# Sliding-window attention with a top-1 mixture of experts on one core: another order of the first steps, another layout of the turned keys and queries, and a later write of empty rows

## The chip, the cores and the metric

One core of a Trainium2 chip runs the whole program. The metric is the device time of one execution in microseconds (us); three timed executions of the kernel before gave 647.55, 648.55 and 649.33 us, median 648.55 us. The engines are named as in the profile: PE (TensorE; PEld is its weight load), DVE (VectorE), ACT (ScalarE), POOL (GpSimd), SP (SyncE, which here only issues DMAs). "SPq" and "ACTq" are rows of DMA issues on these two engines.

## The reference, cut to what matters

```python
# q, k, v: [8 batches, 8 heads, 576 positions, 64]
scores = (q @ k.transpose(0, 1, 3, 2)) / 8
mask   = (rel >= 0) & (rel < 64)            # rel = query position - key position
scores = where(mask, scores, -1e9); scores -= max(scores)
attn   = exp(scores); attn /= sum(attn) + 1e-9
x      = (attn @ v), heads side by side      # 4608 tokens x 512
logits = x @ w_gate + modality_bias[modality_id]
e      = argmax(logits); gate = softmax(logits)[e]
out    = gate * (relu(x @ w1[e]) @ w2[e])    # 8 experts, 512 -> 1024 -> 512
```

## The kernel before, in words

**Tiles and steps.** The 4608 tokens are 72 blocks of 64 positions. One step s of the main loop takes a pair of blocks (128 tokens, 36 pairs) through one stage each: in step s the scores of pair s are formed, the probabilities of pair s-1 are turned, the values of pair s-2 are summed and its result turned, the gate logits of pair s-3 are taken. Since a window reaches back over one block only, a block of queries meets two blocks of keys.

**Turned keys and queries.** Keys and queries are loaded in groups of four blocks (two pairs), turned by PE with an identity matrix into PSUM (L439, called from `heads_t`), and copied by DVE or ACT into `kT` and `qT` (L539, `heads_out`). Both tiles hold eight blocks as a ring: groups alternate between its two halves. Before, their free axes are `[pair of heads, block of the ring, position]`, so that one group's blocks are spread over the whole tile in four pieces. The first group is loaded in two halves (a pair of blocks each, keys by SP, queries by ACT, each in two loads, for even and odd positions) and turned by `first_heads` (copies at L551); `first_pair(0)` stands ahead of the loop, `first_pair(1)` in step 0.

**Order.** The code is scheduled by hand: each engine runs its instructions in the order in which the program issues them, and an engine that waits holds up everything behind it in its own queue. What an instruction waits for is worked out from the tiles that it touches. A step issues, in this order: `values` and `values_out` of pair s-2 (PE L615; DVE reciprocal L621 and product `xa` L623), `logits` of pair s-3 (PE L640, DVE L645), `scores` (PE L563, 16 products into the PSUM tiles `sp0`, `sp1`), `minima` (eight DVE instructions, L577, each adds the mask and takes a row's minimum), `swap_v`, `probs_t` of pair s-1 (PE, copies `pT` by ACT L598), the exponentials (ACT L589, eight, in three lots), `x_t`, the next group's heads in two lots (PE L439 and copies L539), small routing and table instructions on DVE ("ticks"), and the expert weights (`weights`, from step 3: one SP load and its split by ACT L111 and DVE L116).

**swap_v.** The values product needs block 2p-1 and 2p in one tile `ve`: its upper 64 rows are copied by DVE from the pair before (L502), its lower 64 by POOL from this pair (L503). Both copies of pair s-1 are issued in step s behind the minima. `vo`, the loaded values, has three buffers, `ve` two, `sp` and `av` one each.

**Routing.** From step 5 on, every second step routes a group of two pairs: at its end the DVE has the row numbers, and POOL scatters 2 x 128 token rows into `xs_scratch` in DRAM (L716). POOL runs in order too: the scatters stand ahead of the next `ve` copy. From step 12 (`FIRST`) the expert products (L279, L301) are interleaved with the attention steps on PE, and after step 38 they run alone to the end.

**Small inputs.** The modality numbers (`mod_i`, L820), the bias rows (`brow`, L822) and the gate weights (`wg`, L825) are loaded by ACT ahead of its first copy. POOL casts the modality numbers (L912), PE turns them once (the 36-row product of L439, at the end of step 0), DVE copies the result (L916), and POOL forms `bias_sel` from it (L920 to L926), ahead of the first `ve` copy in its queue.

**Empty rows.** Slots without tokens read rows of zeros with an invalid row number. They are written once, 514 KB from the tile `padrow`, by SP at the end of step 2 (L1024).

Of the kernel before, what the change touches and what calls it, by code (L numbers as in the profile page):

```python
# [19 lines left out]
P = 128  # L20
W64 = 64
# [5 lines left out]
def tile_window_attn_moe(  # L27
# [12 lines left out]
    nc = tc.nc  # L40
# [396 lines left out]
    def turn(out_, in_, p0=0):  # L437
        n = in_.shape[0]
        nc.tensor.transpose(out=out_, in_=in_, identity=ident[p0:p0 + n, p0:p0 + n])  # L439
# [11 lines left out]
    small = actx.enter_context(tc.tile_pool(name="small", bufs=2))  # L451


    kT = att.tile([P, HP, RING, W64], F32, name="kT")
    qT = att.tile([P, HP, RING, W64], F32, name="qT")
# [6 lines left out]
    vo = {}  # L462
# [31 lines left out]

    def swap_v(p):

        e = work.tile([P, H, D], F32, name="ve", bufs=2)
        ve[p] = e
        if p == 0:
            nc.gpsimd.memset(e[W64:P], 0.0)  # L500
        else:
            nc.vector.tensor_copy(out=e[W64:P], in_=vo[p - 1][W64:P])  # L502
        nc.gpsimd.tensor_copy(out=e[0:W64], in_=vo[p][0:W64])  # L503

    def new_qk(G, nm):
        if G in AHEAD:
# [27 lines left out]
                turn(tp[:, n * P:(n + 1) * P], src[:, t, 2 * i + h])  # L534

    def heads_out(tp, G, nm, i, copy):
        pos0 = GBLK * (G % 2)
        dst = (qT if nm == "q" else kT)[:, 2 * i:2 * i + 2, pos0:pos0 + GBLK, :]
        copy(out=dst.rearrange("p h j (i t) -> p h t (j i)", t=2),  # L539
             in_=tp.rearrange("p (h t i) -> p h t i", h=2, t=2))  # L540

    def first_heads(nm, i, tp, copy):

        src = qk[0, nm].rearrange("p t (h a) d -> p t h (a d)", a=2)
        rows = slice(i * W64, (i + 1) * W64)
        for h in range(HP):
            for t in range(2):
                n = 2 * h + t
                turn(tp[:, n * W64:(n + 1) * W64], src[rows, t, h], i * W64)
        dst = (qT if nm == "q" else kT)[:, :, 2 * i:2 * i + 2, :]  # L550
        copy(out=dst.rearrange("p h j (i t) -> p h t (j i)", t=2),  # L551
             in_=tp.rearrange("p (h t i) -> p h t i", h=HP, t=2))

    def scores(p):


        g = 2 * p % RING
        win = (slice(g, g - 2 if g else None, -1 if g else RING - 1), slice(g, g + 2))
        sp = [ps_s.tile([P, 512], F32, name=f"sp{a}") for a in range(2)]
        for hp in range(HP):  # L560
            for a, c in ((0, 0), (1, 1), (0, 1), (1, 0)):
                rows = slice(a * W64, (a + 1) * W64)
                nc.tensor.matmul(  # L563
                    out=sp[a][c * W64:(c + 1) * W64, hp * P:(hp + 1) * P], lhsT=qT[rows, hp, g + c, :],
                    rhs=kT[rows, hp, win[c], :], start=True, stop=True)
# [246 lines left out]
    for f, args in at.pop(-1):  # L812
# [7 lines left out]
    nc.scalar.dma_start(out=mod_i, in_=mod_id.bitcast(I32).rearrange("(g x) -> g x", x=2 * P))  # L820
    brow = const.tile([P, 2, E], F32, name="brow")
    nc.scalar.dma_start(  # L822
        out=brow, in_=mod_bias.rearrange("(o m) e -> o m e", o=1).broadcast_to([P, 2, E]))
    wg = const.tile([P, NC1, E], F32, name="wg")
    nc.scalar.dma_start(out=wg, in_=w_gate.rearrange("(c p) e -> p c e", p=P))  # L825
    idle = epool.tile([P, 2 * 512], BF16, name="hh", bufs=2)
    nc.vector.memset(idle[:, 0:512], 0.0)

# [11 lines left out]
    nc.gpsimd.memset(kT[:, :, RING - 1, :], 0.0)  # L840


    masks = const.tile([P, 3, P], F32, name="masks")
# [81 lines left out]
            if m:  # L925
                nc.gpsimd.tensor_tensor(out=bias_sel, in0=bias_sel, in1=dst, op=ALU.add)  # L926

    def first_pair(i):
        for nm in "kq":
            first_heads(nm, i, turn_bank(0), nc.vector.tensor_copy if nm == "k" else nc.scalar.copy)  # L930

    first_pair(0)

    def weights(s):

# [10 lines left out]
    for s in range(NPR + 4):  # L946
        j = s % GB
        for f, args in at.pop(s, ()):
            f(*args)
        n_tick = 6 if s < FIRST else 5  # L950
        n_gap = 0 if s < FIRST else 4
        G = s // GB + 1
        heads = PARTS[j] if G < NG else ()
        R = (s - 5) // GB if s >= 5 and j == 1 else -1

        if 2 <= s < NPR + 2:
            values(s - 2)
            values_out(s - 2)
        if 3 <= s < NPR + 3:
            logits(s - 3, turn_bank(s))  # L960
            if (s - 3) % GB == GB - 1:
                route1((s - 3) // GB)
        if s < NPR:
            scores(s)
            if s == 0:
                keep_warm(WARM[1])
                first_pair(1)
            minima(s)
        if 1 <= s <= NPR:
# [24 lines left out]
        run_later()  # L994
        tick(n_tick)
        cnt = None
        if R >= 0:
            tp = turn_bank(s)
            rk = route2(R, tp)
            if R == NG - 1 or any(R == T for T, _ in EARLY):  # L1000
                cnt = counts_out(tab if R == NG - 1 else pl, counts(R, tp))
            route3(R, rk)
        if s < NPR:
            exps(s, (5, 6, 7))
        if n_gap > 2:
            if FIRST < s < FIRST + 3:
                weights(s)
            gap(it, True)
        if heads:
            tp = turn_bank(s)  # L1010
            heads_t(G, *heads[1], tp)
            heads_out(tp, G, *heads[1], nc.scalar.copy if heads[1] == K1 else nc.vector.tensor_copy)
        run_later()
        tick(n_tick)
        if s >= 3:
            weights(s)
        if n_gap > 3:
            gap(it, True)
        run_later()
        if s == 0:  # L1020
            select_bias()
            choose()
        if s == 2:
            nc.sync.dma_start(out=xs_blk[DUMMY:DUMMY + 2].rearrange("b p c -> p b c"), in_=padrow)  # L1024
# [270 lines left out]
```

## Time and profile before

| what | value |
|---|---|
| median of three runs | 648.55 us (647.55 to 649.33) |
| the profiled execution's own time | 648.28 us |
| its span in the profile | 646.4 us, 1.9 us less than its time |
| PE busy in the span | 620.0 us, 96% |
| DVE, ACT, POOL busy | 367.7 us, 299.4 us, 137.4 us |
| moved by DMA | 88.07 MB |

A row of the timeline gives the start in us from the span's beginning, the duration in us, engine, line, operation, output and inputs with their shapes, and in brackets how long the engine had been idle and what released it. A row of the windows gives, for a stretch, each engine's busy time and number of instructions, the clock that TensorE was granted (1.00 is full), the busy share of the DMA engines and GB/s. Matmuls are pipelined: a row's duration is that of one from start to end, and the next can begin long before.

### The profile page before, as it was taken

Reading aid. Unit: us, or ns where it says so; the run is one execution under the profiler, and the core shown is the slowest. Engines: PE = TensorE matmul, PEld = TensorE weight load, DVE = VectorE, ACT = ScalarE, POOL = GpSimd, SP = SyncE. Lnnn points to the kernel's source line nnn. Section 1 sums busy time; section 2 is a strip of 40 time slices with the busy share of each in tenths; the row PEclk is TensorE's granted clock in tenths of the full one; section 3 lists DMA queues with packets and bytes.
Section 4 is the critical chain, followed back from the end, with each engine's and each line's share of the span. In section 5 each row is a group of like instructions: output and inputs, shape, how many; then the busy total and the mean of one; then the engine's idle time right before and its main releaser. Section 6 shows DMA issues by size and latency. Waiting matters only on the chain.

```text
span 646.4 us, 17286 instructions
## 1 busy us (share of the span) xinstructions
PE 620.0 (96%) x6508; PEld 554.6 (86%) x6509; DVE 367.7 (57%) x1494; ACT 299.4 (46%) x932; POOL 137.4 (21%) x314
## 2 busy tenths in 40 slices
PE   6888889999999999999999999999999999999996
PEld 4677779898989888889998898899898999989986
DVE  2889967777767686766655365122214524757611
ACT  2789875756565646555544111111113513555411
POOL 4315330232142212320322220011011101101102
PEclk9999989999999999999999999999999999999999
DMA  9988975764876754553412124421041732677300
GB/s 164 195 186 216 212 197 132 196 161 120 181 171 153 159 144 103 144 133 82 132 51 83 50 99 171 157 67 66 23 173 45 236 113 85 218 247 227 120 1 36
DMA packets 138885, 88.07 MB, mean 136 GB/s; under 512 B 116746, under 2 KB 116784, under 8 KB 138672
## 3 DMA queue, kind: packets, MB, share of 16 engines
q1 hardware_dynamic: 130112, 67.44, 42.2%
q0 software_dynamic: 5856, 18.92, 7.8%
q10 hardware_dynamic: 2832, 0.59, 0.6%
q8 instruction: 52, 0.85, 0.6%
q14 instruction: 33, 0.27, 0.2%
HBM read 67.49 MB, written 23.91 MB: 141 GB/s over the span
## 4 chain that ended last, share of the span: by engine, by line
PE 50%; DVE 0%; ACT 0%; issue 0%; POOL 0%; POOLq 0%; ACTq 0%
PE y L301 22%; PE em L279 12%; PE sp L279 10%; PE tp L439 1%; PE y L352 1%; PE av L615 1%; PE em L254 1%; PE tp L254 1%; PE sp L327 0%; PE em L327 0%; PE tp L640 0%; PE sp L563 0%; DVE xa L623 0%; ACT ss L589 0%; DVE hl L288 0%
## 5 line engine op out<-in xcount | busy, mean ns | idle before, releaser
L301 PE MATMUL y<-Whi,hh 128*128 128x512 f32 x288 | 118.7, 412 | 0.0
L301 PE MATMUL y<-Wlo,hh 128*128 128x512 f32 x288 | 112.9, 392 | 0.0
L301 PE MATMUL y<-Whi,hl 128*128 128x512 f32 x288 | 112.8, 392 | 0.0
L589 ACT ACTIVATE ss<-ss,mn 128x128 f32<-128x128 f32 x288 | 112.5, 397 | 0.0
L279 PE MATMUL em<-xh,Whi 128*128 128x256 f32 x400 | 103.5, 293 | 1.2 <-ACT xh L192 0.7
L279 PE MATMUL em<-xh,Wlo 128*128 128x256 f32 x400 | 98.5, 280 | 0.0
L288 DVE SCALAR_TENSOR_TENSOR hl<-em,hh 128x512 fp32r<-128x512 f32 x50 | 34.5, 690 | 92.9 <-ACT hh L287 91.3
L312 POOL DMA_INDIRECT out_dram<-y,id x36 | 37.3, 1036 | 224.6 <-DVE y L309 145.9
L279 PEld LDWEIGHTS em<-xh,Whi 128*128 128x128 f32 x400 | 75.9, 190 | 2.6 <-ACT xh L192 0.9
L279 PEld LDWEIGHTS em<-xh,Wlo 128*128 128x128 f32 x400 | 75.8, 190 | 0.9
L287 ACT ACTIVATE hh<-em 128x512 fp32r<-128x512 f32 x50 | 29.6, 592 | 93.3 <-PE em L279 89.4
L577 DVE CUSTOM_DVE_ANT_0 ss<-sp,masks 128x128 f32<-128x128 f32 x288 | 63.5, 286 | 13.4 <-PE sp L563 13.4
L598 ACT COPY pT<-tp 128x512 f32<-128x512 f32 x58 | 32.2, 589 | 78.0 <-PE tp L439 78.0
L301 PEld LDWEIGHTS y<-Whi,hl 128*128 128x128 f32 x288 | 54.1, 188 | 12.3
L279 PE MATMUL em<-xl,Whi 128*128 128x256 f32 x400 | 63.4, 281 | 0.0
L301 PEld LDWEIGHTS y<-Whi,hh 128*128 128x128 f32 x288 | 54.1, 188 | 7.5
L301 PEld LDWEIGHTS y<-Wlo,hh 128*128 128x128 f32 x288 | 54.3, 188 | 7.1
L589 ACT ACTIVATION_READ_ACCUMULATOR ss<-ss,mn 128x1 f32 x288 | 55.8, 194 | 0.0
L716 POOL DMA_INDIRECT xs_scratch<-xa,idx x36 | 36.3, 1007 | 89.1 <-DVE lm L659 26.9
L279 PEld LDWEIGHTS em<-xl,Whi 128*128 128x128 f32 x400 | 54.2, 189 | 0.0
L288 DVE SCALAR_TENSOR_TENSOR hl<-sp,hh 128x512 fp32r<-128x512 f32 x22 | 15.2, 692 | 61.1 <-ACT hh L287 61.1
L615 PEld LDWEIGHTS av<-ve,pT 128*64 128x64 f32 x576 | 36.4, 138 | 15.2 <-issue 7.4
(242 smaller groups left out, 1243.6 us busy)
## 6 DMA issues: line engine op xcount, KB each, us to landing
xt<-xs_scratch SPq DMA_DIRECT2D x18, 514.0 KB, 4.0
vo<-in_v_dram SPq DMA_DIRECT2D x32, 256.0 KB, 4.1
y<-in_moe_w_dram SPq DMA_DIRECT2D x32, 256.0 KB, 4.0
vo<-in_moe_w_dram SPq DMA_DIRECT2D x24, 256.0 KB, 3.5
ss<-in_moe_w_dram SPq DMA_DIRECT2D x24, 256.0 KB, 3.8
qk<-in_k_dram SPq DMA_DIRECT2D x18, 256.0 KB, 5.5
qk<-in_q_dram SPq DMA_DIRECT2D x18, 256.0 KB, 4.9
xs_scratch<-xs_scratch SPq DMA_DIRECT2D x8, 514.0 KB, 6.0
```

Of the source, the lines that this page charges most:

```text
L254: nc.tensor.transpose(out=tp[:, n * P:(n + 1) * P].bitcast(F32R), in_=xt[:, t, c * P:(c + 1) * P].bitcast(F32R), identity=ident_r)
L279: nc.tensor.matmul(out=hb[:, i * TP:(i + 1) * TP], lhsT=w[buf][:, c0:c0 + P], rhs=x[:, c * TP:(c + 1) * TP], start=(n == 0), stop=(n == le ...
L287: nc.scalar.activation(out=hh, in_=hb, func=AF.Relu),
L288: nc.vector.scalar_tensor_tensor(out=hl, in0=hb, scalar=0.0, in1=hh.bitcast(F32), op0=ALU.max, op1=ALU.subtract)))
L301: nc.tensor.matmul(out=sl["y", t], lhsT=h[:, i * TP + t * P:i * TP + (t + 1) * P], rhs=w[buf][:, c0:c0 + DM], start=(k == 0 and n == 0), s ...
L312: ins = nc.gpsimd.indirect_dma_start(out=out, out_offset=bass.IndirectOffsetOnAxis(ap=sl["id"][:, t:t + 1], axis=0), in_=y, in_offset=None ...
L352: nc.tensor.matmul(out=yp[:, cols], lhsT=sl["h", n][lo][:, c * P:(c + 1) * P], rhs=w[buf][:, c0 + cols.start:c0 + cols.stop], start=(m == ...
L577: nc.vector.tensor_tensor_reduce(out=ss[a][:, hp, :], in0=sp[a][:, hp * P:(hp + 1) * P], in1=mask, scale=-1.0 / 8.0, scalar=3.0e38, op0=AL ...
L589: nc.scalar.activation(out=ss[a][:, hp, :], in_=ss[a][:, hp, :], func=AF.Exp, bias=mn[:, h:h + 1], scale=-1.0, accum_out=sm[:, h:h + 1])
L598: nc.scalar.copy(out=pT, in_=pp)
L615: nc.tensor.matmul(out=av[c * W64:(c + 1) * W64, 2 * hp + a], lhsT=pT[:, i:i + W64], rhs=(vo if c else ve)[p][:, 2 * hp + a, :], start=Tru ...
L716: ins = nc.gpsimd.indirect_dma_start(out=xs, out_offset=bass.IndirectOffsetOnAxis(ap=idx[:, j:j + 1], axis=0), in_=xg[j], in_offset=None)
```

## The change

Five things are edited.

1. `kT` and `qT` get the axes `[half of the ring, pair of heads, block of the group, position]`, so that a group is one contiguous half of the tile. `place(g, hp)` gives the position of a block; `win` in `scores` gives the two key blocks.
2. `first_heads` is split in two: the turns are issued by position parity (keys even, queries even, keys odd, queries odd), and for the first pair each copy is cut into halves of two head pairs, the first by DVE, the second by ACT. For the second pair the copies stay whole (keys DVE, queries ACT).
3. In step 0 the second pair's copies stand behind the eight minima (DVE) and behind five of the eight exponentials (ACT), no longer ahead of them. Its turns keep their place on PE.
4. The three small loads are issued by ACT behind the first pair's copies.
5. The upper half of `ve` (`swap_upper`, DVE) is issued at the head of a step, ahead of the reciprocal; the lower half (POOL) keeps its place. The empty rows are written at the end of step 5 in place of step 2.

```diff
-    kT = att.tile([P, HP, RING, W64], F32, name="kT")
+    kT = att.tile([P, 2 * HP * GBLK, W64], F32, name="kT")
+    def place(g, hp):
+        a, j = divmod(g, GBLK)
+        return (a * HP + hp) * GBLK + j
...
     def swap_v(p):
-        e = work.tile([P, H, D], F32, name="ve", bufs=2)
-        ve[p] = e
+        e = ve[p]
         if p == 0:
             nc.gpsimd.memset(e[W64:P], 0.0)
-        else:
-            nc.vector.tensor_copy(out=e[W64:P], in_=vo[p - 1][W64:P])
         nc.gpsimd.tensor_copy(out=e[0:W64], in_=vo[p][0:W64])
+    def swap_upper(p):
+        e = work.tile([P, H, D], F32, name="ve", bufs=2)
+        ve[p] = e
+        if p > 0:
+            nc.vector.tensor_copy(out=e[W64:P], in_=vo[p - 1][W64:P])
...
+    def first_heads_out(nm, i, tp, copies):
+        dst = by_group(qT if nm == "q" else kT)[:, 0, :, 2 * i:2 * i + 2, :]
+        n = HP // len(copies)
+        for c, copy in enumerate(copies):
+            hs = slice(c * n, (c + 1) * n)
+            copy(out=dst[:, hs].rearrange("p h j (i t) -> p h t (j i)", t=2),
+                 in_=tp.rearrange("p (h t i) -> p h t i", h=HP, t=2)[:, hs])
...
-    def first_pair(i):
-        for nm in "kq":
-            first_heads(nm, i, turn_bank(0), nc.vector.tensor_copy if nm == "k" else nc.scalar.copy)
-    first_pair(0)
+    both = nc.vector.tensor_copy, nc.scalar.copy
+    def first_pair(i, copies):
+        tps = [turn_bank(0) for _ in "kq"]
+        for t in range(2):
+            for nm, tp in zip("kq", tps):
+                first_heads_t(nm, i, t, tp)
+        for nm, tp, c in zip("kq", tps, copies):
+            first_heads_out(nm, i, tp, c)
+    first_pair(0, (both, both))
+    nc.scalar.dma_start(out=mod_i, in_=mod_id.bitcast(I32).rearrange("(g x) -> g x", x=2 * P))
+    nc.scalar.dma_start(
+        out=brow, in_=mod_bias.rearrange("(o m) e -> o m e", o=1).broadcast_to([P, 2, E]))
+    nc.scalar.dma_start(out=wg, in_=w_gate.rearrange("(c p) e -> p c e", p=P))
...
+        if 1 <= s <= NPR:
+            swap_upper(s - 1)
         if 2 <= s < NPR + 2:
             values(s - 2)
...
             if s == 0:
                 keep_warm(WARM[1])
-                first_pair(1)
             minima(s)
...
             exps(s, (2, 3, 4))
+        if s == 0:
+            first_pair(1, (both[:1], both[1:]))
...
-        if s == 2:
+        if s == 5:
             nc.sync.dma_start(out=xs_blk[DUMMY:DUMMY + 2].rearrange("b p c -> p b c"), in_=padrow)
```

How the instructions move is shown at three places. The names in brackets are the semaphores that a row waits for, one per engine or DMA lane; DMASW0 and DMASW1 are lanes of POOL's own DMAs.

ACT in step 0, before: the small loads (L820 to L825), the two copies of queries, the exponentials (L589), a copy of the next group's keys.

```order
L820 DMA y<-in_moe_modality_id_dram 36x256 [waits DMAHW1_49]
L822 DMA brow<-in_moe_modality_bias_dram 128x16 [waits DMAHW3_49]
L825 DMA wg<-in_moe_w_gate_dram 128x4x8 [waits DMAHW4_49]
L551 COPY qT<-tp 128x4x2x64 [waits PE_49]
L551 COPY qT<-y_288 128x4x2x64 [waits PE_49]
L589 ACTIVATE ss,sm<-ss,mn 128x128 [waits DVE_49] x8
L539 COPY kT<-tp 128x2x2x128 [waits PE_49,Pool_49]
```

The same stretch of ACT in the changed kernel (L565 are the first group's copies, L610 the exponentials, L549 the next group's copy).

```order
L565 COPY kT<-tp 128x2x2x64 [waits DVE_49]
L565 COPY qT<-tp 128x2x2x64 [waits DVE_49]
L956 DMA y<-in_moe_modality_id_dram 36x256 [waits DMAHW3_49]
L957 DMA brow<-in_moe_modality_bias_dram 128x16 [waits DMAHW4_49]
L959 DMA wg<-in_moe_w_gate_dram 128x4x8 [waits DMAHW6_49]
L610 ACTIVATE ss,sm<-ss,mn 128x128 [waits DVE_49] x5
L565 COPY qT<-y_298 128x4x2x64 [waits PE_49]
L610 ACTIVATE ss,sm<-ss,mn 128x128 [waits DVE_49] x3
L549 COPY kT<-tp 128x2x2x128 [waits PE_49,Pool_49]
```

The loads have moved behind the first copies, whose ACT halves each wait for DVE's half, and five exponentials now stand ahead of the second pair's queries.

PE at the scores of step 1 (16 products that alternate between `sp0` and `sp1`; head pair 0 first), before; the rows left out wait for nothing.

```order
L439 MATMUL tp_331<-ident_r_139,y_126 128x36 [waits Pool_49]
L563 MATMUL sp0_368<-kT_98,qT_99 64x128 [waits DVE_49,Activation_49]
L563 MATMUL sp1_369<-kT_98,qT_99 64x128 [waits DVE_49]
...
L563 MATMUL sp0_368<-kT_98,qT_99 64x128 [waits DVE_49]
...
L563 MATMUL sp0_368<-kT_98,qT_99 64x128 [waits Activation_49]
...
L439 MATMUL em_401<-ident_r_139,ss_298 128x128 [waits PE_49]
```

The same place in the changed kernel.

```order
L439 MATMUL tp_326<-ident_r_136,Whi1_64 128x128 x4
L439 MATMUL tp_333<-ident_r_136,y_126 128x36 [waits Pool_49]
L584 MATMUL sp0_371<-kT_98,qT_99 64x128 [waits DVE_49,Activation_49]
L584 MATMUL sp1_372<-kT_98,qT_99 64x128
...
L439 MATMUL em_403<-ident_r_136,ss_280 128x128 [waits PE_49]
```

The three later waits inside the 16 products are gone. The first of them was for the minima that free `sp1`; those at head pairs 1 and 3 were for copies of the next group's keys (L539, by DVE and by ACT), which these products do not read. The turn of the modality numbers, which waits for POOL's cast, still stands directly ahead.

SP around the write of the empty rows, before: L489 loads values, L524 keys and queries, L1024 is the write.

```order
L489 DMA vo<-in_v_dram 128x8x64 [waits DMAHW1_49]
L524 DMA Whi_64<-in_k_dram 128x8x64 [waits DMAHW2_49]
L524 DMA Whi_64<-in_k_dram 128x8x64 [waits DMAHW3_49]
L1024 DMA xs_scratch<-xt 128x2x514 [waits DMAHW4_49,Pool_49]
L489 DMA vo<-in_v_dram 128x8x64 [waits DVE_49,DMAHW5_49,PE_49,Pool_49]
```

SP around it in the changed kernel (L1054 is the write, L497 loads values, L100 and L104 expert weights, L535 keys).

```order
L100 DMA y<-in_moe_w_dram 128x512 [waits DMAHW5_49]
L1054 DMA xs_scratch<-xt 128x2x514 [waits DMAHW6_49,DMASW1_49,DMASW0_49]
L497 DMA vo<-in_v_dram 128x8x64 [waits DVE_49,DMAHW7_49,PE_49,Pool_49]
L104 ISA
L104 DMA y<-in_moe_w_dram 128x512 [waits DMAHW0_49,DVE_49]
L497 DMA vo<-in_v_dram 128x8x64 [waits DVE_49,DMAHW1_49,PE_49,Pool_49]
L535 DMA qk<-in_k_dram 128x8x64 [waits DMAHW2_49]
```

The write has moved from ahead of the values of pair 3 to ahead of those of pair 6, and it now waits for the two scatters of group 0, which POOL issues in step 5.

More of the change, by code (lines that the diff above doesn't have):

```diff
@@ L451, in tile_window_attn_moe, with by_group @@
     small = actx.enter_context(tc.tile_pool(name="small", bufs=2))
-    kT = att.tile([P, HP, RING, W64], F32, name="kT")
-    qT = att.tile([P, HP, RING, W64], F32, name="qT")
+    kT = att.tile([P, 2 * HP * GBLK, W64], F32, name="kT")
+    qT = att.tile([P, 2 * HP * GBLK, W64], F32, name="qT")
+    def place(g, hp):
+        a, j = divmod(g, GBLK)
+        return (a * HP + hp) * GBLK + j
+    def by_group(x):
+        return x.rearrange("p (a h j) i -> p a h j i", a=2, h=HP)
     pause = att.tile([1, 1], F32, name="pause")
@@ L495, in swap_v @@
     def swap_v(p):
+        e = ve[p]
+        if p == 0:
+            nc.gpsimd.memset(e[W64:P], 0.0)
+        nc.gpsimd.tensor_copy(out=e[0:W64], in_=vo[p][0:W64])
+    def swap_upper(p):
         e = work.tile([P, H, D], F32, name="ve", bufs=2)
         ve[p] = e
-        if p == 0:
-            nc.gpsimd.memset(e[W64:P], 0.0)
-        else:
+        if p > 0:
             nc.vector.tensor_copy(out=e[W64:P], in_=vo[p - 1][W64:P])
-        nc.gpsimd.tensor_copy(out=e[0:W64], in_=vo[p][0:W64])
     def new_qk(G, nm):
@@ L536, in heads_out, with first_heads_t @@
     def heads_out(tp, G, nm, i, copy):
-        pos0 = GBLK * (G % 2)
-        dst = (qT if nm == "q" else kT)[:, 2 * i:2 * i + 2, pos0:pos0 + GBLK, :]
+        dst = by_group(qT if nm == "q" else kT)[:, G % 2, 2 * i:2 * i + 2]
         copy(out=dst.rearrange("p h j (i t) -> p h t (j i)", t=2),
              in_=tp.rearrange("p (h t i) -> p h t i", h=2, t=2))
-    def first_heads(nm, i, tp, copy):
+    def first_heads_t(nm, i, t, tp):
         src = qk[0, nm].rearrange("p t (h a) d -> p t h (a d)", a=2)
@@ L546, in first_heads, with win @@
         for h in range(HP):
[L547 to L552, printed above, removed]
+            n = 2 * h + t
+            turn(tp[:, n * W64:(n + 1) * W64], src[rows, t, h], i * W64)
+    def first_heads_out(nm, i, tp, copies):
[5 more added lines that the diff above has]
+                 in_=tp.rearrange("p (h t i) -> p h t i", h=HP, t=2)[:, hs])
     def scores(p):
         g = 2 * p % RING
-        win = (slice(g, g - 2 if g else None, -1 if g else RING - 1), slice(g, g + 2))
+        def win(c, hp):
+            i = place(g, hp)
+            if c:
+                return slice(i, i + 2)
+            n = place((g - 1) % RING, hp)
+            return slice(i, n + 1 if n > i else n - 1 if n else None, n - i)
         sp = [ps_s.tile([P, 512], F32, name=f"sp{a}") for a in range(2)]
@@ L563, in scores @@
                 nc.tensor.matmul(
-                    out=sp[a][c * W64:(c + 1) * W64, hp * P:(hp + 1) * P], lhsT=qT[rows, hp, g + c, :],
-                    rhs=kT[rows, hp, win[c], :], start=True, stop=True)
+                    out=sp[a][c * W64:(c + 1) * W64, hp * P:(hp + 1) * P], lhsT=qT[rows, place(g + c, hp), :],
+                    rhs=kT[rows, win(c, hp), :], start=True, stop=True)
         st[p, "sp"] = sp
@@ L819, in tile_window_attn_moe @@
     mod_i = spare[0:NPR, 0:2 * P].bitcast(I32)
-    nc.scalar.dma_start(out=mod_i, in_=mod_id.bitcast(I32).rearrange("(g x) -> g x", x=2 * P))
     brow = const.tile([P, 2, E], F32, name="brow")
-    nc.scalar.dma_start(
-        out=brow, in_=mod_bias.rearrange("(o m) e -> o m e", o=1).broadcast_to([P, 2, E]))
     wg = const.tile([P, NC1, E], F32, name="wg")
-    nc.scalar.dma_start(out=wg, in_=w_gate.rearrange("(c p) e -> p c e", p=P))
     idle = epool.tile([P, 2 * 512], BF16, name="hh", bufs=2)
@@ L839, in tile_window_attn_moe @@
     nc.gpsimd.tensor_copy(out=ident_r, in_=ident_0)
-    nc.gpsimd.memset(kT[:, :, RING - 1, :], 0.0)
+    nc.gpsimd.memset(by_group(kT)[:, 1, :, GBLK - 1, :], 0.0)
     masks = const.tile([P, 3, P], F32, name="masks")
@@ L1034, in __init__ @@
         def __init__(self):
-            self.words = kT[0:1].rearrange("p h j i -> p (h j i)")
+            self.words = kT[0:1].rearrange("p c i -> p (c i)")
             self.n = 0
```

## The prediction

> **What bounds the kernel now.** I read the page's busy shares first, then busy time by stretches, then the timeline of the head of the program.
>
> ```profile
> PE 620.0 (96%) x6508; PEld 554.6 (86%) x6509; DVE 367.7 (57%) x1494; ACT 299.4 (46%) x932; POOL 137.4 (21%) x314
> ```
> ```profile
> 16.00:24.00 8.00, 5.79 (x110) 4.42 (x110) 5.44 (x34) 6.57 (x29) 4.97 (x10) 1.00 1.20 202
> 40.00:48.00 8.00, 6.94 (x155) 6.10 (x151) 6.40 (x36) 7.33 (x33) 0.42 (x2) 1.00 0.99 202
> 48.00:64.00 16.00, 13.42 (x248) 11.98 (x250) 15.38 (x82) 15.07 (x59) 8.32 (x14) 1.00 0.82 215
> 96.00:128.00 32.00, 32.00 (x421) 29.03 (x421) 23.81 (x111) 21.65 (x72) 5.48 (x13) 1.00 0.63 161
> ```
>
> From 96 us on PE is busy without a break, and over the whole span it is at 96%, so nearly all its idle time lies ahead of that point. What is done behind it is not changed by the edits, so the time can only come from the stretch ahead of it, and what is won there reaches the end one for one. In 48 to 64 us DVE is busy for 15.38 of 16 us, ACT for 15.07. So the attention steps alone are bound by DVE, with ACT close behind; up to 48 us DVE has holes. The question is which holes close.
>
> **The start.** These rows show the first group: turns on PE, copies on DVE and ACT, scores, minima.
>
> ```profile
> 6.84 1.86 PE L439 MATMUL tp<-ident_r,qk 64*128 64x64 f32 x15 [1.57 <-DMA qk<-in_k_dram]
> 7.88 0.69 DVE L551 COPY kT<-tp 128x512 f32<-128x512 f32 x1 [6.65 <-PE tp L439]
> 8.74 0.61 ACT L551 COPY qT<-tp 128x512 f32<-128x512 f32 x1 [3.63 <-PE tp L439]
> 9.45 1.99 PE L563 MATMUL sp<-kT,qT 64*64 64x128 f32 x32 [0.75 <-ACT qT L551]
> 12.20 0.63 PE L832 MATMUL em<-hh 128*128 128x512 bf16 x1 [0.22 <-issue]
> 13.69 0.69 DVE L551 COPY kT<-em 128x512 f32<-128x512 f32 x1 [5.12 <-PE em L439]
> 14.30 0.28 DVE L577 CUSTOM_DVE_ANT_0 ss<-sp,masks 128x128 f32<-128x128 f32 x1
> 17.81 0.60 ACT L539 COPY kT<-tp 128x512 f32<-128x512 f32 x1
> 18.46 0.45 PE L563 MATMUL sp<-kT,qT 64*64 64x128 f32 x8 [1.07 <-ACT kT L539]
> 18.97 0.29 DVE L577 CUSTOM_DVE_ANT_0 ss<-sp,masks 128x128 f32<-128x128 f32 x1 [2.20 <-PE sp L563]
> ```
>
> Three losses are seen. The scores of step 0 end at 9.45 + 1.99 = 11.44, yet the minima begin at 14.30, since DVE first waits for the second pair's keys (13.69). The last products of step 1 wait for a copy of the next group's keys on ACT (17.81 + 0.60), which they don't read; DVE is idle for 2.20 us behind them. And all 15 later turns follow a load that came at 6.84.
>
> *New start.* Of the 16 turns only the odd halves follow that load: eight instead of 15, at 1.86 / 15 = 0.12 each, so keys are ready near 7.5 and queries near 7.9. Copies in halves: an estimate from 0.69 and 0.61 for whole ones is 0.40 each, and ACT's half waits for DVE's. Keys 7.5 to 8.35; DVE's half of the queries 7.95 to 8.4. The first products need these, and start near 8.5, not 9.45; they end near 10.5. The minima follow at once: eight, from 10.5 to 12.2 (14.30 to 15.98 before). The three idle products that follow the scores and the second pair's 16 turns move up as PE does, by 0.95: the idle products ended at 12.20 + 0.63 = 12.83, now near 11.9. Five exponentials are done on ACT before the second pair's queries are turned, so that copy isn't late.
>
> *The guard in PE's queue.* Directly ahead of the scores of step 1 stands the turn of the modality numbers, whose load is now issued behind ACT's copies, near 8.9.
>
> ```profile
> 3.99 0.59 ACTq L820 DMA_DIRECT2D y<-in_moe_modality_id_dram  x1
> 10.20 0.29 POOL L912 CAST y<-y 36x128 f32<-36x128 int32 x1 [1.05 <-DMA y<-in_moe_modality_id_dram]
> brow<-n_moe_modality_bias_dram ACTq DMA_DIRECT2D x1, 8.0 KB, 4.9
> wg<-in_moe_w_gate_dram ACTq DMA_DIRECT2D x1, 16.0 KB, 4.4
> 15.11 0.25 PE L439 MATMUL tp<-ident_r,y 36*128 36x36 f32 x1
> ```
>
> The last row is the turn itself. The load took 10.20 - 3.99 = 6.2 us, behind queries in its own queue; the two small loads after it took 4.9 and 4.4. Now that queue is nearly empty: I take 4.9, landing at 13.8 and cast by 14.1; with 6.2 it is 15.4. PE came to that turn at 15.11; moved up by between 0 and 0.95 it comes there between 14.2 and 15.1, and I take 14.6, as the second pair's loads may hold its turns. So the scores of step 1 start at 14.8 (at worst 15.6), last 1.1, and the minima start at 15.9 (16.7), not 18.97. **Gain 3.05 us, at worst 2.3.** From the minima to the end of step 3 I see no hole in DVE that could take this back: POOL's work on the bias follows the same turn, and the loads of the next groups landed 1 to 2 us ahead of the new need.
>
> **Steps 4 and 5.**
>
> ```profile
> 36.53 0.29 DVE L577 CUSTOM_DVE_ANT_0 ss<-sp,masks 128x128 f32<-128x128 f32 x1 [0.57 <-PE sp L563]
> 41.63 0.59 ACT L539 COPY kT<-em 128x512 f32<-128x512 f32 x1
> 42.27 0.45 PE L563 MATMUL sp<-kT,qT 64*64 64x128 f32 x8 [0.97 <-ACT kT L539]
> 42.88 0.29 DVE L577 CUSTOM_DVE_ANT_0 ss<-sp,masks 128x128 f32<-128x128 f32 x1 [1.25 <-PE sp L563]
> 33.20 0.42 DVE L502 COPY ve<-vo 64x512 f32<-64x512 f32 x1
> 33.77 0.24 PE L615 MATMUL av<-ve,pT 128*64 128x64 f32 x1 [0.78 <-DVE ve L502]
> ```
>
> In step 5 the same false wait (41.63 + 0.59 = 42.22) costs DVE 1.25. The layout removes it. In step 4 PE was late by 0.78, since the values waited for DVE's half of `ve` (33.20 + 0.42); at the head of a step this copy is done some 5 us earlier. DVE's hole there is 0.57. Moving the copy costs DVE nothing (the same 0.42, elsewhere); it delays `xa` by 0.45 within a step, which falls into PE's slack. **Gain 0.57 + 1.25 = 1.8 us**, 1.2 if ACT, 94% busy from 48 us, can't follow all of it.
>
> **The empty rows.** At step 2 their write cost nobody anything: DVE has no hole there. At step 5 it is a new plug: SP holds it until group 0's scatters have landed, and the values of pair 6, two weight pieces and keys stand behind it.
>
> ```profile
> 49.89 0.97 POOL L716 DMA_INDIRECT xs_scratch<-xa,idx  x1 [0.28 <-POOL xa L715]
> DMA to landing us min/median/max: 3.0/3.5/6.3
> 45.27 0.39 SPq L489 DMA_DIRECT2D vo<-in_v_dram  x1
> vo<-in_v_dram SPq DMA_DIRECT2D x1, 256.0 KB, 3.2
> DMA to landing us min/median/max: 4.5/4.5/4.5
> 23.21 1.11 SPq L1024 DMA_DIRECT2D xs_scratch<-xt  x1
> 51.93 0.61 POOL L503 COPY ve<-vo 64x512 f32<-64x512 f32 x1
> 57.04 0.24 PE L615 MATMUL av<-ve,pT 128*64 128x64 f32 x1
> 58.62 1.10 PE L563 MATMUL sp<-kT,qT 64*64 64x128 f32 x32
> 60.50 0.28 DVE L577 CUSTOM_DVE_ANT_0 ss<-sp,masks 128x128 f32<-128x128 f32 x1
> ```
>
> In the clock of before (all of it moves up together): the second scatter lands at 49.89 + 3.0 to 3.5 = 52.9 to 53.4 (the first landing row, that of L716); the write is issued in 0.4 to 1.1; the values of pair 6 go out then, not at 45.27, and land 3.2 later if alone, 4.5 as the write itself did (the second landing row): 56.9 to 59.4, I take 58.3. POOL copies them (0.61, before at 51.93, so the order on POOL holds until then), and PE can form the values of step 8 at 58.95, not 57.04. Its scores (58.62 + 1.10) have 1.2 us of slack to the minima (60.50, now 0.45 later by the moved copy). **Cost 1.9 - 1.2 = 0.7 us, from 0 to 1.8.**
>
> **Sum.** 3.05 + 1.8 - 0.7 = 4.2 us (rounded up by under 0.1), from 2.3 + 1.2 - 1.8 = 1.7 to 4.9. The profiled execution took 648.28, so 644.1 by its own clock; the median of the runs is 0.27 above it, so **644.3 us**. A difference of 0.3%, 1.95 us, is about what a measurement of this kernel can tell from none: below 646.6 is faster, above 650.5 slower.
>
> **The clock.** One stretch ahead of the bound part ran at half clock:
>
> ```profile
> 91.00:92.00 1.00, 0.36 (x1) 0.78 0.97 363
> 92.00:93.00 1.00, 1.00 (x6) 0.50 0.63 143
> 93.00:94.00 1.00, 1.00 (x7) 0.50 0.64 220
> 94.00:95.00 1.00, 1.00 (x6) 0.51 0.98 215
> ```
>
> It follows a stretch with little work on PE, and takes 0.22 + 0.50 + 0.50 + 0.49 = 1.7 us of full-rate time. The step structure there stays, so I leave it in; whether it recurs is a rival. The Trainium skill ("TensorE: Matmul & The Clock Gate", Part 1: The HAM clock gate) says that the clock is set anew by activity windows of about 3.4 us that run free of the kernel's start. By that rule a move of 4 us could drop this window or add one; the trace agrees with the length (0.78 to 0.51 in the rows make about 3.4 us).
>
> **The rivals.**
>
> 1. *The new plug on SP costs more than everything gains: slower.* For: the scatters' longest landing is 6.3, which puts the write at 56.2, the values of pair 6 at 56.2 + 1.1 + 0.4 + 4.5 = 62.2 and the cost at 62.2 + 0.65 - 57.04 - 1.2 = 4.6: no gain left, 648.3. The group's keys for step 8 stand behind it; each further us moves the end as much. From a landing of about 64.5 on it is slower by over 0.3%; with 2.5 us more, 650.8. Against: the typical landing is 3.5, and no other SP row needs more than 4.5. Chance 0.04 slower, 0.06 for a cost of 3 to 4.6 (647 to 648.3).
> 2. *ACT becomes the bound.* It is 94% busy from 48 us; if it can't follow, steps 4 and 5 give nothing and 3.05 - 0.7 = 2.35 is left: 646.2. Against: ACT still waits for PE in these steps. Chance 0.12.
> 3. *The loads don't keep up with the earlier start* (DMA engines 1.20 busy at 16 to 24 us), or the modality numbers land late by 2 us more: 2 us less, 646.4. Chance 0.06.
> 4. *The half-clock stretch goes, or a second one comes:* 1.7 us less or more, 642.6 or 646.0. Chance 0.05 each.
>
> The forecast itself has 0.62. The range, 642.2 to 646.8, takes in the sum's own bounds (643.7 to 646.8), cases 2 to 4 and a little more gain than seen; beyond it lie case 1 and larger surprises. Faster: 0.60 + 0.12 + 0.10 and about 0.02 of case 3, 0.84. Same: 0.06 of case 1, 0.04 of case 3, 0.02 of the forecast's upper end, 0.12. Slower: 0.04.
>
> **What would show it.** Right: first minima near 10.5, those of step 1 near 16; no product of scores waiting for ACT's L549; PE saturated some 4 us earlier; the values of pair 6 issued behind the scatters' landing, with a DVE hole of up to 2 us in step 8. Wrong: a PE wait for POOL's cast ahead of step 1 of over 1 us, a hole in DVE at step 6 to 8 of 3 us or more, or the minima of step 5 still behind an idle time.

## The result, and the profile after

| | before | after |
|---|---|---|
| median of 13 runs each, one beside the other | 648.2 us (646.75 to 652.16) | 652.4 us (650.24 to 657.05) |
| ratio after / before, 95% interval | | 1.0066 (1.005 to 1.0083) |
| span of the profiled execution | 646.4 us | 650.7 us |

The change makes the kernel slower by 0.66%; the forecast was 644.3 us, 0.65% faster. So some 8 us have to be found: a gain that came and was lost, and a loss on top.

First the lead, read where DVE starts the reciprocal of a step (steps 7, 9, 13 and 36 here; start in us, duration, engine, line). The kernel before:

```profile
53.71 0.20 DVE L621 RECIPROCAL rs<-rs 128x8 f32<-128x8 f32 x1
65.35 0.20 DVE L621 RECIPROCAL rs<-rs 128x8 f32<-128x8 f32 x1
97.50 0.19 DVE L621 RECIPROCAL rs<-rs 128x8 f32<-128x8 f32 x1
345.31 0.19 DVE L621 RECIPROCAL rs<-rs 128x8 f32<-128x8 f32 x1
```

The kernel after, the same four:

```profile
49.64 0.20 DVE L642 RECIPROCAL rs<-rs 128x8 f32<-128x8 f32 x1
64.93 0.20 DVE L642 RECIPROCAL rs<-rs 128x8 f32<-128x8 f32 x1
98.36 0.20 DVE L642 RECIPROCAL rs<-rs 128x8 f32<-128x8 f32 x1
349.61 0.20 DVE L642 RECIPROCAL rs<-rs 128x8 f32<-128x8 f32 x1
```

The differences are -4.07, -0.42, +0.86 and +4.30 us, and +4.3 is also the difference of the spans. So most of the forecast gain (3.05 + 1.8 = 4.85 ahead of the empty rows) was there in step 7; 3.65 went between steps 7 and 9, 1.28 by step 13, and 3.44 in the interleaved steps, where nothing was expected to change.

**The start** came as forecast up to the minima of step 1 (10.5 and 15.9 were forecast; before, 14.30 and 18.97). First minima of steps 0 and 1 in the timeline after:

```profile
10.71 0.29 DVE L598 CUSTOM_DVE_ANT_0 ss<-sp,masks 128x128 f32<-128x128 f32 x1 [2.30 <-PE sp L584]
15.50 0.29 DVE L598 CUSTOM_DVE_ANT_0 ss<-sp,masks 128x128 f32<-128x128 f32 x1 [0.85 <-PE sp L584]
```

**Steps 7 to 9.** These are rows of the timeline after, from four engines:

```profile
45.62 0.96 POOL L737 DMA_INDIRECT xs_scratch<-xa,idx  x1 [0.28 <-POOL xa L736]
50.17 0.40 SPq L1054 DMA_DIRECT2D xs_scratch<-xt  x1
50.74 0.39 SPq L497 DMA_DIRECT2D vo<-in_v_dram  x1
54.97 0.81 POOL L508 COPY ve<-vo 64x512 f32<-64x512 f32 x1 [7.44 <-DMA vo<-in_v_dram]
55.84 0.27 PE L636 MATMUL av<-ve,pT 128*64 128x64 f32 x1 [3.51 <-POOL ve L508]
58.12 1.88 PE L584 MATMUL sp<-kT,qT 64*64 64x128 f32 x32
60.05 0.29 DVE L598 CUSTOM_DVE_ANT_0 ss<-sp,masks 128x128 f32<-128x128 f32 x1 [1.66 <-PE sp L584]
```

Read from top to bottom, each waits for the one above: the second scatter, the write of the empty rows behind it (50.17 - 45.62 = 4.55 later), the load of the values of pair 6, POOL's copy, the values product, the scores, the minima. The scores took 1.88 us, not 1.10: PE had stood idle for 3.51 us and ran at half clock. The window of that microsecond shows the granted clock as the third number from the end, 0.50:

```profile
58.00:59.00 1.00, 1.00 (x20) 0.98 (x22) 0.35 (x2) 0.00 (x0) 0.83 (x1) 0.50 1.25 302
```

**The bound part.** Windows of the kernel after, with PE's busy time first (the first three rows answer to rows shown of before):

```profile
16.00:24.00 8.00, 4.83 (x88) 4.12 (x87) 6.98 (x37) 5.26 (x21) 3.83 (x8) 1.00 1.05 197
48.00:64.00 16.00, 12.49 (x243) 11.59 (x241) 11.94 (x63) 11.56 (x48) 4.92 (x9) 0.89 0.85 211
96.00:128.00 32.00, 31.89 (x420) 28.75 (x419) 23.64 (x109) 21.64 (x73) 5.44 (x13) 1.00 0.68 170
128.00:400.00 272.00, 267.05 (x3223) 239.42 (x3222) 170.71 (x841) 134.87 (x462) 66.66 (x134) 1.00 0.47 119
```

and one window of the kernel before:

```profile
128.00:400.00 272.00, 270.23 (x3249) 242.88 (x3248) 175.22 (x846) 135.23 (x462) 66.70 (x135) 1.00 0.48 124
```

From 128 to 400 us PE is idle for 272 - 267.05 = 4.95 us, before for 1.77. The waits of PE from 96 us on name the reason (total, times, longest, in us); after:

```profile
PE tp L439 <- DVE lg L666: 4.1, 5, 1.3
PE tp L439 <- ACT pT L619: 0.7, 1, 0.7
```

and before:

```profile
PE tp L439 <- DVE lg L645: 1.3, 3, 0.7
```

One such wait in the timeline, step 17 after, DVE and PE:

```profile
141.83 0.42 DVE L514 COPY ve<-vo 64x512 f32<-64x512 f32 x1
142.29 0.20 DVE L642 RECIPROCAL rs<-rs 128x8 f32<-128x8 f32 x1
142.58 0.69 DVE L644 TENSOR_TENSOR xa<-av,rs 128x512 f32<-128x512 f32 x1
143.19 0.15 DVE L666 TENSOR_TENSOR lg<-tp,bias_sel 128x8 f32<-128x8 f32 x1
...
140.49 0.59 PE L661 MATMUL tp<-wg,xaT 128*64 128x8 f32 x16
142.05 0.66 PE L439 MATMUL tp<-ident_r,ss 128*128 128x128 f32 x4
143.40 0.66 PE L439 MATMUL tp<-ident_r,ss 128*128 128x128 f32 x4 [0.70 <-DVE lg L666]
```

From step 11 on PE's turns have two banks (`turn_bank` gives out `tp` alone). The logits take one, the first four turns of probabilities the other, and the next four need the first again: it is free when DVE's `lg` has read it. DVE comes to `lg` behind `ve`, the reciprocal and `xa`, and a copy of 0.42 us ahead of these makes it late by as much. It does not show in every step: in step 16 DVE is at `lg` by 131.76, and eight turns follow from 131.49 without a break. In step 17 three longer rows (of the expert products and of a weight piece, 139.65 to 141.80) stand ahead of the copy. The idle times of PE of over 0.6 us come four steps apart, ahead of rows at 143.40, 187.32, 231.86, 275.77 and 319.71, with one more at 350.55. In the same step of the kernel before the eight turns are one row, with an idle time of 0.13 us inside it:

```profile
142.17 0.15 DVE L645 TENSOR_TENSOR lg<-tp,bias_sel 128x8 f32<-128x8 f32 x1
...
141.59 1.45 PE L439 MATMUL tp<-ident_r,ss 128*128 128x128 f32 x8
```

**The clock.** After has the half-clock stretch in step 8 shown above, and another here:

```profile
80.00:81.00 1.00, 0.72 (x4) 0.73 (x5) 0.93 (x10) 1.00 (x6) 0.00 (x0) 0.62 1.16 229
81.00:82.00 1.00, 0.61 (x5) 0.26 (x3) 0.58 (x2) 1.00 (x4) 0.00 (x0) 0.50 0.36 63
...
87.00:88.00 1.00, 1.00 (x25) 0.83 (x18) 0.40 (x3) 0.00 (x0) 0.90 (x1) 0.97 1.37 217
```

With the rows between, all at 0.50, this makes 0.76 + 6 + 0.06 = 6.8 us at half clock, twice the 3.4 us stretch of the kernel before (91 to 95 us), which after has not.

### The profile page after: what moved, and what is told of

The parts are those of the page before. It is cut to its first block, busy times and chain, and to the rows that moved or that the text cites. A ratio compares the mean times of both kernels' runs of the same rounds, so it can differ in the third digit from the quotient of the medians.

```text
span 650.7 us, 17259 instructions
## 1 busy us (share of the span) xinstructions
PE 621.5 (96%) x6509; PEld 556.5 (86%) x6509; DVE 366.5 (56%) x1495; ACT 299.5 (46%) x933; POOL 135.5 (21%) x314
## 5 line engine op out<-in xcount | busy, mean ns | idle before, releaser
L610 ACT ACTIVATE ss<-ss,mn 128x128 f32<-128x128 f32 x288 | 112.6, 398 | 4.1 <-DVE mn L598 4.1
L610 ACT ACTIVATION_READ_ACCUMULATOR ss<-ss,mn 128x1 f32 x288 | 56.0, 194 | 0.0
```

Source lines behind the costliest of these rows:

```text
L610: nc.scalar.activation(out=ss[a][:, hp, :], in_=ss[a][:, hp, :], func=AF.Exp, bias=mn[:, h:h + 1], scale=-1.0, accum_out=sm[:, h:h + 1])
```

## The experiments

The theory (A): two of the edits cost more than the others gain, at two places. The write of the empty rows plugs SP in step 5, and the copy of `ve` at the head of a step holds up PE in the interleaved steps. Against it: the clock alone (B), a hole that is filled later anyway (C), the new layout as the source of the drift (D).

Each kernel was timed beside the kernel before on the same chip (medians of before 648.2 to 649.4; the chips are not the same for all rows). PE's idle time is that from 128 to 400 us of the profiled execution.

| kernel | ratio to before, 95% interval | PE idle, us |
|---|---|---|
| changed | 1.0066 (1.005 to 1.0083) | 4.95 |
| changed, rows at step 2 | 1.0023 (1.0004 to 1.0043) | 4.90 |
| changed, `ve` behind the minima | 0.9992 (0.9976 to 1.0008) | 1.95 |
| both undone | 0.9939 (0.9916 to 0.9961) | 1.76 |
| rows at step 2, `ve` at the head in steps 1 to 11 | 0.9969 (0.9948 to 0.999) | 1.78 |
| rows at step 2, `ve` at the head from step 12 on | 1.0012 (0.9996 to 1.0029) | 4.95 |
| rows at step 2, `ve` behind `lg` | 0.9925 (0.9901 to 0.9949) | 1.75 |
| `ve` behind the minima, rows in step 5 free of the scatters | 0.9957 (0.994 to 0.9974) | 1.78 |
| before, `ve` at the head | 1.0071 (1.005 to 1.0092) | 4.95 |
| before, rows in step 5 | 1.0029 (1.0013 to 1.0045) | 1.78 |
| before, layout alone | 0.996 (0.9945 to 0.9975) | 1.75 |
| before, order of the start alone | 0.9964 (0.9944 to 0.9984) | 1.77 |
| changed, both costs mended in place | 0.9907 (0.9887 to 0.9926) | 1.93 |

**Rows back at step 2.**

```diff
-        if s == 5:
+        if s == 2:
             nc.sync.dma_start(out=xs_blk[DUMMY:DUMMY + 2]...
```

> The changed kernel with the empty rows written at step 2 again, all else as changed. Theory A (two costs, in two places): the write in step 5 plugs SP and costs the 3.65 us by which the lead over the kernel before shrank between steps 7 and 9 (4.07 to 0.42); the copy of ve at the head of a step costs another 3.2 us from step 13 on, every fourth step about 0.65. So this kernel gains 3.65: near 648.8, ratio to before 1.001 (0.998 to 1.003), with a lead of 3.5 to 4 us still there at step 9, and the drift behind step 13 unchanged. Rival B (the clock alone: two half-clock windows more, 1.7 us each, wherever they fall): the ratio follows the count of windows and not the edit; 652 with three windows, 649 with one. Rival C (the hole is filled later, since PE is the bound from step 12 on): 652, ratio 1.006.

Measured 650.32 us, 1.0023: 0.0043 of the time, 2.8 us, is given back. The lead at step 9 is 3.33 us, a little under the 3.5 to 4 expected, and the drift is the same (from -0.22 in step 14 to +3.06 in step 36). C falls. Of the lead 0.71 went between steps 7 and 8 at a wait that the changed kernel does not have: DVE's product `xa` needs a buffer that an earlier scatter still reads.

```profile
50.89 0.69 DVE L644 TENSOR_TENSOR xa<-av,rs 128x512 f32<-128x512 f32 x1 [0.93 <-DMA xs_scratch<-xa,idx]
```

In this execution 3.3 us went between steps 11 and 13, with half-clock stretches from 77 to 84 us and from 91 to 94 us: so its span gained less than its head.

**`ve` behind the minima again.**

```diff
-        if 1 <= s <= NPR:
-            swap_upper(s - 1)
         if 2 <= s < NPR + 2:
             values(s - 2)
...
         if 1 <= s <= NPR:
+            swap_upper(s - 1)
             swap_v(s - 1)
```

> The changed kernel with DVE's half of ve copied behind the minima again, as before the change; empty rows still in step 5. Theory A: the drift of 3.2 us from step 13 on goes, the plug stays: near 649 (648 to 650), ratio 1.001; PE's waits for DVE's lg fall from 4.1 us to the 1.3 of the kernel before, but PE waits for ve in step 4 again (0.6). Rival D (the drift comes from the layout by groups or from loads that fall elsewhere, not from the place of the copy): 652, ratio 1.006, waits for lg as in the changed kernel. Rival B: as the windows have it.

Measured 648.68 us, 0.9992; PE's idle time falls to 1.95 and its waits for `lg` to 1.6 us. D falls: the layout is the new one here. The lead drops by 2.56 us from step 8 to step 9, as the plug is still in.

**Both undone.**

> Both undone: only the layout, the first heads as they arrive and the minima ahead of the second pair are left of the change. Theory A: the gains of the start and of step 5 are kept and both costs are gone: 645.3 (644.3 to 646.5), ratio 0.9955, faster than the kernel before. Rival D: 649. Rival B: 645 to 650 by the number of windows.

Measured 644.87 us, 0.9939. What is left, edits 1 to 4, gains 4.0 us (2.5 to 5.5), and this is the first kernel faster than before. With the four kernels of this square the costs are read twice: the rows 0.0043 with the copy at the head and 0.0053 without (2.8 and 3.4 us), the copy 0.0074 with the rows in step 5 and 0.0084 without (4.8 and 5.4 us). Each of these is uncertain by some 1.5 to 2 us, by the intervals of its two ratios. Together the two costs are 8.2 us, which turn the gain of 4.0 into the measured loss of 4.2.

**`ve` at the head in steps 1 to 11 only.**

```diff
-        if 1 <= s <= NPR:
+        if 1 <= s < FIRST:
             swap_upper(s - 1)
...
         if 1 <= s <= NPR:
+            if s >= FIRST:
+                swap_upper(s - 1)
             swap_v(s - 1)
```

> Empty rows at step 2, and the copy of ve at the head of a step only in steps 1 to 11, behind the minima from step 12 on. Theory A: as with both undone, 645 (644 to 646); whether the copy at the head is worth anything in the head steps is read against that kernel: by the forecast 0.57 us (step 4), by the first trace of the changed kernel perhaps less than nothing, since in step 2 the copy took 0.84 and the reciprocal was late behind it. Rival D: 649.

Measured 645.93 us, 0.9969, no different from both undone within the intervals; the drift is gone (+0.71 in step 13, +0.72 in step 36). No net gain of the head's place is seen in the first steps. Here too a long half-clock stretch (78 to 85 us) followed.

**`ve` behind the sum of the logits.**

```diff
         if 3 <= s < NPR + 3:
             logits(s - 3, turn_bank(s))
...
+        if 1 <= s <= NPR:
+            swap_upper(s - 1)
         if s < NPR:
             scores(s)
             minima(s)
```

> Empty rows at step 2; DVE's half of ve is copied behind the sum of the logits (lg) and ahead of the scores' minima, in every step. It tells why the copy at the head of a step costs. If it is the two banks (lg empties the bank that PE's next turns need, and the copy stands ahead of lg): PE's idle time from 128 to 400 us is that of both undone (1.8 us, not 4.9), and the ratio is near that kernel's 0.994 (0.991 to 0.997). If it is DVE's time ahead of the minima and exponentials as such, the idle time stays near 4.9 and the ratio near 1.002, that of the kernel with rows at step 2 and the copy at the head.

Measured 642.95 us, 0.9925. The copy takes DVE's time ahead of the minima in this kernel too, and PE is not held up: for PE's idle time only its place against `lg` counts. Its window:

```profile
128.00:400.00 272.00, 270.25 (x3182) 242.93 (x3181) 169.12 (x823) 132.52 (x453) 67.15 (x137) 1.00 0.50 130
```

and its waits of PE from 96 us on, those of the kernel before to a tenth:

```profile
PE tp L439 <- DVE lg L666: 1.3, 3, 0.7
```

**Rows in step 5, free of the scatters** (with `ve` behind the minima).

```diff
-            nc.sync.dma_start(out=xs_blk[DUMMY:DUMMY + 2]...
+            ins = nc.sync.dma_start(out=xs_blk[DUMMY:DUMMY + 2]...
+            tc.declare_no_dep(ins.ins, group="scatter", reason="rows that no token has")
```

> The copy of ve behind the minima; empty rows in step 5, but their write is declared free of the scatters, whose rows are others, so SP needn't wait for these to land. It tells the wait from the transfer. If the cost of step 5 is the wait in SP's queue: near both undone, ratio 0.994 (0.991 to 0.997), and no hole in step 8 of DVE. If it is the place of the transfer itself (its 0.4 to 1.2 us of issue, and its bytes beside the loads): as the kernel with only the copy put back, ratio 0.999, with the lead over the kernel before lost by 2.5 us between steps 8 and 9.

Measured 645.02 us, 0.9957, against 0.9992 with the wait in. The write goes out as it is reached and the values of pair 6 right behind it, 8 us earlier than in the changed kernel; SP's issues in the timeline:

```profile
41.05 0.69 SPq L100 DMA_DIRECT2D y<-in_moe_w_dram  x1
41.78 0.43 SPq L1052 DMA_DIRECT2D xs_scratch<-xt  x1
42.39 0.40 SPq L497 DMA_DIRECT2D vo<-in_v_dram  x1
```

There is no hole of DVE in step 8. So the cost was the wait in the queue and not the transfer or its step, as far as the intervals tell: 0.9957 and the 0.9939 of both undone overlap. This execution still loses 0.96 us of its lead between steps 7 and 8, where DVE starts `xa` 1.06 us late (51.12), about when the second scatter lands (51.21); the kernel with the rows at step 2 has such a wait too.

**The kernel before with one edit each.** `ve` at the head:

> The kernel before with one edit: DVE's half of ve copied at the head of each step. If the place of the copy costs whatever the rest is: PE's idle time from 128 to 400 us rises from 1.8 to near 4.9, ratio 1.005 (1.003 to 1.008); the wait of PE for ve in step 4 goes, which can give back 0.6. If the drift needs the new layout beside it: 0.999 to 1.001.

Measured 652.45 us, 1.0071 (4.1 us by the medians), idle time 4.95: the copy alone makes the kernel as slow as the whole change does. It needs no new layout. Rows in step 5:

> The kernel before with one edit: the empty rows written in step 5. By the forecast of the plug in the clock of before 0.7 us (0 to 1.8), ratio 1.001; by what the changed kernel lost between steps 7 and 9 up to 3.6 us, ratio 1.0055. Between these stands the 2.5 us lost there when only the copy was put back, ratio 1.004, which I take: the loads of pair 6 stand behind the scatters' landing whatever the start was, but the kernel before gets to step 8 some 4 us later and so waits less for them, which speaks for the low side.

Measured 650.53 us, 1.0029, 2.2 us above the median of before there (648.33). The write waits until 54.67, the values of pair 6 go out at 55.24 and are copied at 59.49; from step 7 to step 10 this execution loses 2.5 us. Layout alone:

> The kernel before with one edit: keys and queries by group outside and pairs of heads inside. By the terms of the forecast the scores no longer wait for ACT's copies of the next group's keys: the 1.25 us of DVE ahead of the minima of step 5 goes, and ahead of the minima of step 1 some 1.1 of the 2.20 (the wait of PE for that copy was 1.07). Together 2.3 us, ratio 0.9965 (0.995 to 0.998). If the start is bound by its loads instead, only the 1.25 of step 5 comes: 0.998. If neither is worth anything at the end: 1.000.

Measured 646.0 us, 0.996. The lead grows by 1.11 from step 5 to 6, where 1.25 was forecast. Ahead of that it is only 0.24, though the minima of step 1 start at 17.71 and not at 18.97: that gain is lost again in step 2. Another 1.16 comes at step 13, as this execution has no half-clock stretch. The order of the start alone:

> The kernel before with the edits of the start alone: the first heads in the order they arrive, copies in halves, minima of step 0 ahead of the second pair's turns, small loads behind. The layout is that of before, ve and the empty rows too. The minima of step 0 start near 10.8 and not 14.3; those of step 1 still wait for the copy of the next group's keys. If the order of the start is the larger part of what both undone gained (4.0 us): 2.5 to 3 us, ratio 0.9958. If the layout is, and the start is bound at step 1 by the copy: 1 us or less, 0.9985 to 1.000.

Measured 646.33 us, 0.9964, with minima of step 0 at 10.76 and those of step 1 at 18.13. In this profiled execution its lead is 0.33 up to step 12 and 1.49 from step 13; the runs as a whole gain more than the execution that is seen. In that execution PE came to full clock late (17.94 us, before 13.06; see the last section), which may be why. Layout and start alone gain 0.0040 and 0.0036, in sum 0.0076; both undone, which has both, gains 0.0061. The intervals are too wide to call either the larger.

**Both costs mended in place**: `ve` behind `lg`, the rows in step 5 free of the scatters.

> The changed kernel with the copy of ve behind the sum of the logits and ahead of the minima, and with the empty rows in step 5 but free of the scatters. If the two mends add to what the change gained at the start: as with the copy behind lg and the rows at step 2, ratio 0.9925 (0.989 to 0.996), 643 us. If the empty rows' place at step 2 was what made that one good: 0.996 or more.

Measured 642.69 us, 0.9907 (0.9887 to 0.9926): the fastest of all by its ratio, though its interval and that of the kernel with the rows at step 2 overlap.

**`ve` at the head from step 12 on only.**

```diff
-        if 1 <= s <= NPR:
+        if FIRST <= s <= NPR:
             swap_upper(s - 1)
...
         if 1 <= s <= NPR:
+            if s < FIRST:
+                swap_upper(s - 1)
             swap_v(s - 1)
```

> Empty rows at step 2; the copy of ve at the head of a step from step 12 on only, behind the minima in steps 1 to 11. If the cost of the head's place lies in the interleaved steps, this kernel has PE's idle time of 4.9 us from 128 to 400 us, and is 3.2 us longer than the one with both undone: ratio 0.9985 (0.9965 to 1.0005), no more half-clock windows than that one had. If the place in steps 1 to 11 makes the half-clock windows near 80 us, as in the three traces that had it and two of them, none is seen there. If the cost lies in the head steps after all: 0.994.

Measured 649.41 us, 1.0012, above the expected range (0.9965 to 1.0005), though its interval (0.9996 to 1.0029) reaches into it; no half-clock stretch in the profiled execution. The lead falls from 4.10 us in step 11 to 0.77 in step 36, by 3.3 us, with the idle time of the changed kernel in the window from 128 to 400 us:

```profile
128.00:400.00 272.00, 267.05 (x3162) 239.62 (x3161) 168.69 (x829) 134.02 (x460) 67.76 (x136) 1.00 0.47 121
```

and the same waits of PE from 96 us on:

```profile
PE tp L439 <- DVE lg L666: 4.1, 5, 1.3
PE tp L439 <- ACT pT L619: 0.7, 1, 0.7
```

With the kernel that has the copy at the head in steps 1 to 11 only, this places the drift in the interleaved steps.

## Why the prediction was wrong

**The step that failed**: "Moving the copy costs DVE nothing (the same 0.42, elsewhere); it delays `xa` by 0.45 within a step, which falls into PE's slack", together with "What is done behind 96 us is not changed by the edits". The copy stands in the loop and so in the steps from 12 on too, where PE is the bound and has no slack but for 1.8 us in all, part of it at this very wait (1.3 us for `lg` in the kernel before). The delay was looked at for `xa` alone; the row behind it on DVE, `lg`, empties a bank for which PE waits. Worth 3.1 to 3.2 us of idle PE in each of the four traces that have the copy at the head of the late steps, 4.1 us as an edit alone (1.0071) and 4.8 to 5.4 in the square. What makes up the difference is not shown; the uncertainty of some 1.5 to 2 us covers most of it. The waits of PE in the trace of before showed it: 1.3 us, three times, was the sign that `lg` had no room.

**Empty rows, 0.7 (0 to 1.8)**: the mechanism was right, the size was not. Alone it cost 2.2 us, in the changed kernel 2.8 to 3.4. The chain in the changed kernel: the write starts at 50.17, which is 54.24 in the clock of before (lead 4.07), where 52.9 to 53.4 had been forecast, as the second scatter took 4.5 us and not 3.0 to 3.5; the load of the values goes out at 50.74, there 54.81, where 53.3 to 54.5 had been forecast. The values product starts at 55.84, 2.87 later than 57.04 - 4.07 = 52.97, where 1.9 was forecast. Then 1.2 of slack was to be taken off. Instead the stretch from values to the end of the scores took 60.00 - 55.84 = 4.16 us, not 59.72 - 57.04 = 2.68, since PE at half clock followed the idle time: 1.48 more. 2.87 + 1.48 - (60.50 - 59.72) = 3.57, and the minima are late by 60.05 - (60.50 - 4.07) = 3.62. So in this execution a hole in PE cost its own length and the clock behind it. It need not: in the kernel before with the rows in step 5 PE stands idle for 2.19 us at the same place (60.15), and from 60 to 68 us the clock is full. The rival that named this plug was right as a mechanism, with 4.6 as its price, and had 0.04 and 0.06. Its counter-argument, that no other SP row needs more than 4.5 us, misread the trace of before: key loads of 256 KB there have a median of 5.5.

**Start, 3.05**: minima of step 1 at 15.50 (forecast 15.9). Of these 3.47 us, 1.48 was left in step 3: in step 2 POOL's copy waits 2.03 us for its load and DVE's reciprocal for POOL behind it, which is the rival of loads that don't keep up. DVE's own copy of `ve` stands ahead of that reciprocal too, ends at the same time (22.21) and took twice its usual 0.42 us there, so the two are not told apart. Which executions keep how much varies (below).

**Steps 4 and 5, 1.25 for the false wait**: right; 1.11 with the layout alone, and no scores wait for ACT's copy after. **0.57 for `ve` in step 4**: there, but not kept. From step 4 to 5 the lead grows by 0.77 to 0.81 us in the four traces that have the copy at the head there, and by -0.24 to 0.18 in the seven that have it behind the minima. Between the minima of step 1 and step 3, though, the three with the copy at the head and the new start lose 1.3 to 2.0 us of lead, those with it behind the minima at most 0.9. That fits the delay by the copy, but no run takes these first steps apart.

**Sum of start and layout**: with both costs undone the copy's 0.57 is out, so 3.05 + 1.25 = 4.3 was forecast, and 4.0 (2.5 to 5.5) measured.

**Clock**: one stretch was left in, one more was priced at 1.7. The price was right: of the runs of before beside the first four experiments, the 19 with a mean granted clock of 0.996 have a median of 648.99 us, the 7 with 0.998 or 0.999 of 647.24, 1.75 less. After had one or two more: nine of its 13 runs are at 0.992 or 0.993. B alone doesn't explain the result: the idle time of PE from 128 to 400 us is all at full clock. That the head copy in steps 1 to 11 brings the stretch near 80 us stays open: the three profiled executions with it and the new layout have one of 6.8 us, that of the kernel before with the copy at the head has none.

## What to carry to other kernels

An instruction moved to the head of an in-order queue delays every instruction behind it in every turn of the loop: list who waits for each of those, in the stage that is the bound, and look first at the waits that are already there, however short. A DMA that must wait for another engine's DMA belongs last in its queue, or, if its bytes are others, needs a declaration that it is independent: here the load behind it went out 8 us later. And an edit that serves the start of a loop should be tried in those steps alone.

## What was not expected of the hardware

PE's full clock comes at two times in the start, for the same instructions. Both undone, PE:

```profile
13.98 1.11 PE L439 MATMUL y<-ident_r,Whi 128*128 128x128 f32 x4
14.88 1.06 PE L439 MATMUL tp<-ident_r,Whi 128*128 128x128 f32 x4
```

`ve` behind `lg`, the same turns:

```profile
13.07 0.65 PE L439 MATMUL y<-ident_r,Whi 128*128 128x128 f32 x4
13.56 0.60 PE L439 MATMUL tp<-ident_r,Whi 128*128 128x128 f32 x4
```

The start is the same code in both, and the minima of step 1 begin at 17.67 in the one and 15.43 in the other, 2.24 us apart: as large as an edit's worth. The granted clock of the windows reads 1.00 in both, but it has no entry there: the trace's first entry of the clock, at full rate, begins at 16.97 us in the one and at 11.66 in the other, and the windows count what lies ahead as full. Of the 14 profiled executions nine have that entry between 11.6 and 13.8 us, before and after among them, and five between 16.9 and 18.5: both undone, `ve` at the head in steps 1 to 11, and before with `ve` at the head, with the rows in step 5 and with the order of the start. Of the kernels with layout and start together, the seven of the first kind have the minima of step 1 at 15.43 to 15.81, the two of the second at 17.67 and 17.90. So the lead of an execution of the second kind is some 2 us too low from its first steps on (an estimate from these minima), and only its changes from step to step can be read. The Trainium skill ("TensorE: Matmul & The Clock Gate", Part 1: The HAM clock gate) says that the activity window runs free of the kernel's start, so that the number of matmuls at the low clock differs from run to run; that it differs agrees with these times.

Where DVE's copy of `ve` and POOL's meet, it is mostly the one that starts second that is longer. In step 2 of the changed kernel POOL was first, and DVE took 0.84 us in place of 0.42:

```profile
21.32 0.60 POOL L508 COPY ve<-vo 64x512 f32<-64x512 f32 x1 [2.03 <-DMA vo<-in_v_dram]
...
21.37 0.84 DVE L514 COPY ve<-vo 64x512 f32<-64x512 f32 x1
```

In the kernel before, DVE was first here, and POOL took 0.85 us in place of 0.60:

```profile
88.03 0.42 DVE L502 COPY ve<-vo 64x512 f32<-64x512 f32 x1
88.06 0.85 POOL L503 COPY ve<-vo 64x512 f32<-64x512 f32 x1
```
